# Deeper rings in a linear-attention and gated-convolution kernel: four output buffers, four gates, three x chunks

## The chip, the cores and the metric

The kernel runs on one NeuronCore of a Trainium2 chip. The metric is the time of one execution on the device in microseconds; the median of several runs is compared.

## The reference

All arrays are float32 (the weights of the second block arrive as float64). The first block is a linear attention without softmax, normalised per head; the second one multiplies a value projection by a gate that is the sigmoid of a causal depthwise convolution over time, and projects the product once more.

```python
# q, k, v: (8 batches, 8 heads, 576 tokens, 64)
kv = einsum('bhsd,bhse->bhde', k, v)
o = einsum('bhsd,bhde->bhse', q, kv)
o = o / sqrt(mean(o*o, axis=-1) + 1e-6) * g_norm
x = o.transpose(0, 2, 1, 3).reshape(8, 576, 512)
xp = concatenate([zeros((8, 4, 512)), x], axis=1)
gate = sigmoid(sum(conv_w[t] * xp[:, t:t+576] for t in range(5)))
out = (gate * (x @ w_val)) @ w_out
```

## The kernel before

**Order.** The whole order is written out by hand in the string `PLAN`: some 1,240 steps such as `normalise 3 1`, each a small function of a batch `b` (0 to 7) and a piece of it. The program records the steps in that order, so each engine and each DMA queue runs its own instructions in that order; a tile framework adds the semaphore waits. Nothing is reordered at run time. Batches overlap: while one is projected, the next is in its gate and the one after is loaded.

**One batch.** `load_half` and `load_q` bring k, v and q on SyncE's queue (SP). `kv_product` makes the 64x64 products of k and v, `kv_copy` takes them out of PSUM. `raw_pair` and `raw_tail` multiply the turned q with them; five chunks `c` of tokens result (four of 128 and a tail). `square` (ScalarE), `sums` (VectorE, DVE) and `powers` (GpSimd) make the norm, and `normalise` writes the chunk into a tile `x`: 8 (for the tail 4) ScalarE instructions at L592, for batch 0 one of DVE. The chunk then goes into the transposed array `xT`: for batches 0, 1 and for the tail by PE (`turn_x`) and ScalarE (`keep_x`), otherwise by DVE's 32x32 transposes (`turn_blocks`, L617) and DMAs (`move_blocks`, L625, four a step, half on SP's queue and half on GpSimd's). A buffer of `x` is free again after `turn_x` or `turn_blocks`. `halo` (GpSimd, L632) copies the causal margin inside `xT`.

**Gate.** For each of four blocks `jt` of 128 channels, `gate_start` (ScalarE, L636) writes a new tile `gate`, four `gate_tap` (DVE, L642) add the taps of the convolution, `gate_end` (ScalarE, L649) applies the sigmoid, and `gated` (DVE, L667) multiplies it into the value projection that lies in `gv`. After `gated` the buffer is free.

**Projections.** `val_fast` and `val_keep` make the value projection, by a scheme of seven half-size products in place of eight; the sums that it needs are made by `x_sums` (DVE, L688). The output projection is made by the same scheme: `token_sums` (DVE, L773), `fast_product` (PE, L795) and `fast_keep`, which takes the products out of PSUM into a tile `ot`: ScalarE copies first (L807, L809, L811, L818), and DVE adds the rest (L805). The last 64 tokens of two batches go by `out_product` (PE, L741) and `keep_out` (ScalarE, L749). `store` (L827) sends each `ot` tile out in four DMAs of 64 KB on SP's queue; the buffer is free when they have landed.

**Weights.** They arrive as float64 and are narrowed in the first 70 us by `narrow_weight`; its parts 5 and 6 (DVE, L382 and L387) use buffers of the same ring `ot` as scratch, and part 7 (DVE, L391) is the last reader.

**Rings.** A tile is taken with `work.tile(..., tag=..., bufs=n)`: tiles of one tag share `n` buffers. When a tile is taken, it gets the buffer that has been free for longest in the order of the steps, and its first writer waits for the last user of the tile that held that buffer. So the depth of a ring changes no order, only which earlier instruction the first writer must wait for.

Of the kernel before, what the change touches and what calls it, by code (L numbers as in the profile page):

```python
# [9 lines left out]
FP32 = mybir.dt.float32  # L10
U32 = mybir.dt.uint32
# [4 lines left out]
P = 128  # L16
# [193 lines left out]
def kernel(  # L210
# [13 lines left out]
    C = H * D  # L224
# [17 lines left out]
    FAST_VAL = 2  # L242
    FAST_OUT = 0
    ROOTS = {(0, 2): H + H // 2, (0, 1): 2 * H}
    GATES = 3
    GVS = 3
    assert NJ == 4 and NB == 18
    assert 2 * T == P and NB * TB == S and SV <= 512 and C <= 512 and D == 2 * TB
# [3 lines left out]
    work = ctx.enter_context(tc.tile_pool(name="work", bufs=2))  # L252
# [45 lines left out]
    st = {}  # L298
# [51 lines left out]
    def narrow(key, dst, n):  # L350


        w = staged[key]
        rows, size = w.shape[0], w.shape[1]
        split = lambda a: a if len(dst.shape) == 2 else a.rearrange(
            "p (m c) -> p m c", m=dst.shape[1])
        lo, hi = w[:, :, 0], w[:, :, 1]
        if n in (0, 5, 6):
            tag, kind, bufs = {0: ("wexp", U32, 2), 5: ("ot", U32, 3), 6: ("ot", FP32, 3)}[n]
            staged[key, n] = work.tile(  # L360
                [P, C], kind, tag=tag, bufs=bufs, name=f"{tag}{n}_{key[0]}{key[1]}")[0:rows, 0:size]
        e, m, mf = (staged.get((key, part)) for part in (0, 5, 6))

        if n == 0:
            nc.vector.tensor_scalar(
                out=e, in0=hi, scalar1=20, scalar2=0x7FF,
                op0=ALU.logical_shift_right, op1=ALU.bitwise_and,
            )
        elif n == 1:
            nc.scalar.activation(out=e, in_=e, func=AF.Relu, bias=biases[0:rows, 0:1])  # L370
        elif n == 2:
            nc.scalar.activation(out=e, in_=e, func=AF.Relu, bias=biases[0:rows, 1:2], scale=-1.0)
        elif n == 3:
            nc.scalar.activation(
                out=e, in_=e, func=AF.Identity, bias=biases[0:rows, 2:3], scale=-float(1 << 23))
        elif n == 4:
            nc.vector.scalar_tensor_tensor(
                out=e, in0=hi, scalar=0x80000000, in1=e, op0=ALU.bitwise_and, op1=ALU.bitwise_or,
            )
        elif n == 5:  # L380

            nc.vector.tensor_scalar(  # L382
                out=m, in0=hi, scalar1=0xFFFFF, scalar2=1 << 20,
                op0=ALU.bitwise_and, op1=ALU.bitwise_or,
            )
        elif n == 6:
            nc.vector.scalar_tensor_tensor(  # L387
                out=mf, in0=lo, scalar=2.0 ** -32, in1=m, op0=ALU.mult, op1=ALU.add,
            )
        else:  # L390
            nc.vector.scalar_tensor_tensor(  # L391
                out=dst, in0=split(mf), scalar=gcol[:] if key[0] == "wval" else 2.0 ** -20,
                in1=split(e.bitcast(FP32)),
                op0=ALU.mult, op1=ALU.mult,
            )
# [15 lines left out]
    def narrow_weight(*key):  # L411
        narrow(key[0:2], weights[key[0:2]][3], key[2])
# [130 lines left out]
    def heads(c):  # L543
        return H if c < NJ else H // 2
# [30 lines left out]

    def normalise(b, c):
        n = heads(c)
        x = work.tile([P, C], FP32, tag="x", bufs=2, name=f"x{b}_{c}")
        st["x", b, c] = x
        root = st["rt", b][:, FIRST[c]:FIRST[c] + n]  # L580
        if b in WHOLE:
            nc.vector.tensor_tensor(
                out=x[:, 0:n * D].rearrange("p (r h e) -> p r h e", r=2, e=D),
                in0=st["raw", b, c][:].rearrange("p (h r e) -> p r h e", r=2, e=D),
                in1=root.rearrange("p (h r) -> p r h", r=2).unsqueeze(3).broadcast_to((P, 2, n // 2, D)),
                op=ALU.mult)
            return
        for r, raw in enumerate(st["raw", b, c]):
            if b in ACT_NORM:
                for h in range(n // 2):  # L590
                    to = r * n // 2 + h
                    nc.scalar.activation(  # L592
                        out=x[:, to * D:(to + 1) * D], in_=raw[:, h * D:(h + 1) * D], func=AF.Copy,
                        scale=root[:, to:to + 1])
                continue
            nc.vector.tensor_tensor(
                out=x[:, r * n // 2 * D:(r + 1) * n // 2 * D].rearrange("p (h e) -> p h e", e=D),
                in0=raw.rearrange("p (h e) -> p h e", e=D),
                in1=root[:, r * n // 2:(r + 1) * n // 2].unsqueeze(2).broadcast_to((P, n // 2, D)), op=ALU.mult)
# [34 lines left out]
    def gate_start(b, jt):  # L634
        gate = work.tile([P, S], FP32, tag="gate", bufs=GATES, name=f"gate{b}_{jt}")
        nc.scalar.activation(  # L636
            out=gate[:], in_=xTs[b % 2][:, jt, HALO:SX], func=AF.Copy, scale=cwT[:, K - 1, jt:jt + 1])
        st["gate", b, jt] = gate
# [106 lines left out]
        st["po", i, c] = po  # L745

    def keep_out(i, c):
        ot = work.tile([P, C], FP32, tag="ot", bufs=3, name=f"ot{i}_{c}")
        nc.scalar.copy(out=ot[:], in_=st["po", i, c][:])  # L749
        st["ot", i, c] = ot  # L750

# [47 lines left out]
    def fast_keep(i, p, n):  # L799
        a, b, c = (st.get((bank, i, p)) for bank in "abc")  # L800
        row = int(n in (1, 4, 6))
        if ("ot", i, 2 * p + row) not in st:
            st["ot", i, 2 * p + row] = work.tile([P, C], FP32, tag="ot", bufs=3, name=f"ot{i}_{2 * p + row}")
        first, second = (st.get(("ot", i, 2 * p + r)) for r in range(2))
        add = lambda out, one: nc.vector.tensor_tensor(out=out, in0=one, in1=out, op=ALU.add)  # L805
        if n == 0:
            nc.scalar.copy(out=first[:, LOW], in_=a)  # L807
        elif n == 1:
            nc.scalar.copy(out=second[:, HIGH], in_=c)  # L809
        elif n == 2:  # L810
            nc.scalar.copy(out=first[:, HIGH], in_=a)  # L811
        elif n == 4:
            add(second[:, HIGH], a)
        elif n == 5:
            add(first[:], st["bc", i, p][:].rearrange("p r c -> p (r c)"))
        else:
            last = (i, p) == (B // 2 - 1, 2 * NV - 1)
            (nc.vector.tensor_copy if last else nc.scalar.copy)(out=second[:, LOW], in_=a)  # L818
# [4 lines left out]
    def store(i, c, queue=nc.sync, blocks=range(HB)):  # L823
# [5 lines left out]
    steps = {f.__name__: f for f in (  # L829
        load_half, load_q, load_q_rows, stage_weight, narrow_weight, turn_cw, keep_cw, start_warm, warm_up,  # L830
        kv_product, kv_half, kv_copy, turn_q, turn_q_rows, sort_q, raw_half, raw_pair, raw_tail, square, sums, powers, normalise,
        turn_x, keep_x, turn_blocks, move_blocks, halo, gate_start, gate_tap, gate_end, val_product, keep_val, gated,
        val_sums, x_sums, val_fast, val_keep, out_product, keep_out, weight_sums, token_sums, fast_product, fast_keep,
        store, store_last)}
    with tc.manual_schedule():
# [34 lines left out]
```

## Time and profile before

| | |
|---|---|
| runs shown, median (lowest to highest) | 305.32 us (304.0 to 305.74) |
| the profiled execution, time | 305.54 us |
| its span (first to last instruction) | 303.8 us |
| TensorE: matmuls (PE), weight loads (PEld) | 293.9 us, 226.6 us busy |
| VectorE (DVE) | 273.0 us busy |
| ScalarE (ACT) | 194.4 us busy |
| GpSimd (POOL) | 114.5 us busy |
| DMA | 55.51 MB, mean 183 GB/s |

The profile is of one execution. Its own time is 1.74 us longer than its span. Busy times of engines overlap, so they don't add up to the span. A wait is written with the instruction that waits, an arrow, and the last instruction that it waited for; three numbers behind it are the microseconds in total, how often, and the longest. `SPq` and `PEq` are an engine's queue rather than its arithmetic; "issue" is time in which an engine waited for nothing that the profile shows.

### The profile page before, as it was taken

What the parts mean: (1) busy time and instruction counts of PE and PEld (TensorE: products, weight loads), DVE (VectorE), ACT (ScalarE), POOL (GpSimd) and SP (SyncE); (2) the same over time, 40 slices, a digit from 0 to 9 for tenths busy, and PEclk for the clock granted to TensorE, in tenths of its full rate; (3) what the DMA queues carried; (4) which work ended last, traced back from release to release, by engine and by line L of the source; (5) the groups of instructions that cost most, each with busy time, mean ns of one, the idle gap of its engine ahead of it and who ended that gap; (6) DMA issues with size and microseconds to landing.
All of it is one profiled execution on the core that took longest, in us unless ns stands there. A gap on an engine that the chain in (4) does not pass through costs nothing.

```text
span 303.8 us, 8778 instructions
## 1 busy us (share of the span) xinstructions
PE 293.9 (97%) x3333; PEld 226.6 (75%) x3333; DVE 273.0 (90%) x482; ACT 194.4 (64%) x606; POOL 114.5 (38%) x127
## 2 busy tenths in 40 slices
PE   7998999999999999999999999999999999999993
PEld 4787777777887885777778757787877578888582
DVE  1699999999999999999999999999999999999612
ACT  2799989989568654983586537682888354534220
POOL 3047074326549036265328452245535613000000
PEclk9999999999999999999999999999999999999997
DMA  7999995277559776988589477937411621112423
GB/s 269 397 398 340 271 296 144 58 242 223 165 134 332 212 187 147 286 233 247 153 249 299 125 175 214 311 101 222 108 38 37 175 68 36 35 46 61 104 69 104
DMA packets 32073, 55.51 MB, mean 183 GB/s; under 512 B 6166, under 2 KB 14358, under 8 KB 32032
## 3 DMA queue, kind: packets, MB, share of 16 engines
q1 hardware_dynamic: 29520, 49.76, 56.6%
q0 software_dynamic: 1632, 3.17, 4.0%
q10 hardware_dynamic: 880, 2.03, 1.8%
q8 instruction: 26, 0.43, 0.6%
q14 instruction: 15, 0.12, 0.1%
HBM read 39.21 MB, written 9.44 MB: 160 GB/s over the span
## 4 chain that ended last, share of the span: by engine, by line
PE 76%; DMA 8%; SPq 5%; ACT 4%; DVE 3%; issue 2%; DVEq 0%
PE a L795 15%; PE va L703 13%; PE cb L795 12%; PE val L654 11%; PE vc L703 6%; PE kvps L445 4%; PE raw L521 4%; DMA out_dram<-ot 4%; PE out L741 4%; PE vb L703 3%; DMA qs<-in_q_dram 3%; SPq L625 2%; PE xTps L604 2%; DMA v<-in_v_dram 2%; SPq L322 1%
## 5 line engine op out<-in xcount | busy, mean ns | idle before, releaser
L573 POOL TENSOR_TENSOR rt<-ss,mhalf 128x8 f32<-128x8 f32 (+3 forms) x38 | 68.5, 1810 | 101.0 <-DVE ss L565 100.8
L642 DVE SCALAR_TENSOR_TENSOR gate<-xT,cwT,gate 128x576 f32<-128x576 f32 x128 | 101.8, 809 | 1.0
L592 ACT ACTIVATE x<-raw,rt 128x64 f32<-128x64 f32 x252 | 55.9, 353 | 6.9 <-POOL rt L573 4.1
L625 POOL DMA_DIRECT2D xT<-y x48 | 26.4, 557 | 25.9 <-DVE ot L805 14.4
L654 PE MATMUL val<-xT,wval 128*128 128x288 f32 x128 | 33.4, 412 | 0.0
L795 PE MATMUL a<-wsum,sums 128*128 128x256 f32 x128 | 32.5, 383 | 0.0
L649 ACT ACTIVATE gate<-gate 128x576 f32<-128x576 f32 x32 | 22.0, 692 | 12.1 <-DVE gate L642 11.9
L654 PEld LDWEIGHTS val<-xT,wval 128*128 128x128 f32 x128 | 23.5, 190 | 6.9 <-DVE wval L391 0.5
L795 PEld LDWEIGHTS a<-wsum,sums 128*128 128x128 f32 x128 | 23.9, 190 | 4.4 <-issue 0.6
L556 ACT ACTIVATE sq<-raw 128x256 f32<-128x256 f32 (+1 forms) x70 | 22.1, 402 | 7.8 <-PE raw L521 7.5
L703 PE MATMUL va<-xs,vsum 128*128 128x288 f32 x96 | 26.6, 409 | 0.0
L636 ACT ACTIVATE gate<-xT,cwT 128x576 f32<-128x576 f32 x32 | 25.2, 810 | 1.4 <-DVE gv L667 1.3
L565 DVE TENSOR_REDUCE ss<-sq 128x8 f32<-128x520 f32 (+1 forms) x40 | 24.7, 627 | 0.8 <-ACT sq L556 0.7
L667 DVE TENSOR_TENSOR gv<-gv,gate 128x576 f32<-128x576 f32 x32 | 23.6, 750 | 0.9 <-ACT gate L649 0.8
L703 PEld LDWEIGHTS va<-xs,vsum 128*128 128x128 f32 x96 | 18.0, 190 | 5.2 <-ACT x L592 0.4
L632 POOL COPY xT<-xT 128x124 f32<-128x124 f32 x32 | 17.5, 585 | 10.9 <-ACT xT L611 10.9
L521 PEld LDWEIGHTS raw<-kv,qT 64*64 64x64 f32 x1008 | 16.7, 134 | 6.4 <-issue 3.5
L521 PE MATMUL raw<-kv,qT 64*64 64x64 f32 x1008 | 19.0, 221 | 0.9 <-DVE gv L710 0.6
L445 PEld LDWEIGHTS kvps<-v,k 64*64 64x64 f32 x1008 | 15.8, 135 | 4.1 <-issue 2.9
L445 PE MATMUL kvps<-v,k 64*64 64x64 f32 x1008 | 17.4, 220 | 0.0
L470 DVE STREAM_TRANSPOSE qT<-qs 128x512 f32<-128x512 f32 x24 | 16.6, 693 | 0.5 <-DMA qs<-in_q_dram 0.5
L805 DVE TENSOR_TENSOR ot<-cb,ot 128x512 f32<-128x512 f32 x16 | 10.9, 681 | 6.8 <-DMA out_dram<-ot 4.1
(114 smaller groups left out, 545.5 us busy)
## 6 DMA issues: line engine op xcount, KB each, us to landing
qs<-in_q_dram SPq DMA_DIRECT2D x96, 140.0 KB, 4.6
out_dram<-ot SPq DMA_DIRECT2D x140, 64.0 KB, 1.7
k<-in_k_dram SPq DMA_DIRECT2D x14, 576.0 KB, 6.7
v<-in_v_dram SPq DMA_DIRECT2D x12, 576.0 KB, 7.0
xT<-y SPq DMA_DIRECT2D x48, 64.0 KB, 2.7
xT<-y POOLq DMA_DIRECT2D x48, 64.0 KB, 3.1
y<-in_moe_w_val_dram SPq DMA_DIRECT2D x4, 512.0 KB, 11.4
w_wout<-in_moe_w_out_dram SPq DMA_DIRECT2D x4, 512.0 KB, 7.1
```

What stands on the lines that cost most here:

```text
L445: nc.tensor.matmul(st["kvps", b][s][r * D:(r + 1) * D, i], st["k", b, i][rows, r, cols], st["v", b, i][rows, r, cols], start=(j == 0), sto ...
L521: nc.tensor.matmul(st["raw", b, c][r][cols, to * D:(to + 1) * D], st["qT", b][rows, hp, first:first + D], kvs[b % 2][rows, hp, :], start=T ...
L565: nc.vector.reduce_sum(out=st["ss", b][:, FIRST[c]:FIRST[c] + n], in_=st["sq", b, c][:, 0:n], axis=AX.X)
L573: nc.gpsimd.tensor_tensor(out=st["rt", b][:, which], in0=st["ss", b][:, which], in1=mhalf[:, which], op=ALU.pow)
L592: nc.scalar.activation(out=x[:, to * D:(to + 1) * D], in_=raw[:, h * D:(h + 1) * D], func=AF.Copy, scale=root[:, to:to + 1])
L625: (nc.sync if i % 2 else nc.gpsimd).dma_start(out=xTs[b % 2][i * TB:(i + 1) * TB, :, first:first + P], in_=y[a * TB:(a + 1) * TB, i])
L636: nc.scalar.activation(out=gate[:], in_=xTs[b % 2][:, jt, HALO:SX], func=AF.Copy, scale=cwT[:, K - 1, jt:jt + 1])
L642: nc.vector.scalar_tensor_tensor(out=gate[:], in0=xTs[b % 2][:, jt, tap * TB:tap * TB + S], scalar=cwT[:, tap, jt:jt + 1], in1=gate[:], op ...
L654: nc.tensor.matmul(val[:], wval[:, kc, jt * P:(jt + 1) * P], xTs[b % 2][:, kc, HALO + n * SV:HALO + (n + 1) * SV], start=(kc == 0), stop=( ...
L667: nc.vector.tensor_tensor(out=both, in0=both, in1=st["gate", b, jt][:], op=ALU.mult)
L703: nc.tensor.matmul(st[bank, "val", b, mj][:], weights_[:, k], tokens()[:, k], start=(n in (0, 1, 3) and k == 0), stop=(k == NK // 2 - 1), ...
L795: nc.tensor.matmul(st[bank, i, p], tokens()[:, k], weights_[:, k], start=(n < 2 and k == 0), stop=(k == NK // 2 - 1), skip_group_check=True)
```

## The change

Three rings get one buffer more each: `gate` has four in place of three, `x` three in place of two, `ot` four in place of three (in all four places where a tile of that tag is taken). No step is moved, and every engine keeps its instructions and their order. The buffers take 6,400 more bytes of each SBUF partition; the tiles that lie behind them in the same pool move up by so much.

```diff
-    GATES = 3
+    GATES = 4
...
-            tag, kind, bufs = {0: ("wexp", U32, 2), 5: ("ot", U32, 3), 6: ("ot", FP32, 3)}[n]
+            tag, kind, bufs = {0: ("wexp", U32, 2), 5: ("ot", U32, 4), 6: ("ot", FP32, 4)}[n]
...
-        x = work.tile([P, C], FP32, tag="x", bufs=2, name=f"x{b}_{c}")
+        x = work.tile([P, C], FP32, tag="x", bufs=3, name=f"x{b}_{c}")
...
-        ot = work.tile([P, C], FP32, tag="ot", bufs=3, name=f"ot{i}_{c}")
+        ot = work.tile([P, C], FP32, tag="ot", bufs=4, name=f"ot{i}_{c}")
...
-            st["ot", i, 2 * p + row] = work.tile([P, C], FP32, tag="ot", bufs=3, name=f"ot{i}_{2 * p + row}")
+            st["ot", i, 2 * p + row] = work.tile([P, C], FP32, tag="ot", bufs=4, name=f"ot{i}_{2 * p + row}")
```

## The prediction

> **What bounds the kernel now.** I read the page first, part 1 and the chain in part 4, then the windows, then the list of waits engine by engine, and last the timeline around each wait that a ring can have caused.
>
> ```profile
> PE 293.9 (97%) x3333; PEld 226.6 (75%) x3333; DVE 273.0 (90%) x482; ACT 194.4 (64%) x606; POOL 114.5 (38%) x127
> ...
> PE 76%; DMA 8%; SPq 5%; ACT 4%; DVE 3%; issue 2%; DVEq 0%
> ```
>
> TensorE fills 97% of the span and carries 76% of the chain that ended last. ScalarE, which makes the first write of nearly every tile whose ring grows, is busy for 64% and has 4% of the chain. The windows show whether that average hides a stage with another limit (columns: stretch, its length, then busy time of PE, PEld, DVE, ACT, POOL):
>
> ```profile
> 30.00:60.00 30.00, 29.99 (x464) 23.02 (x463) 29.82 (x51) 28.22 (x84) 11.05 (x9) 1.00 0.71 191
> ...
> 240.00:270.00 30.00, 30.00 (x133) 23.54 (x130) 28.98 (x45) 13.31 (x32) 5.80 (x8) 1.00 0.25 67
> ...
> sum 268.00, PE 266.44 PEld 206.31 DVE 252.47 ACT 173.33 POOL 102.78; mean PE 29.60 PEld 22.92 DVE 28.05 ACT 19.26 POOL 11.42
> ```
>
> From 30 to 298 us PE is busy for 266.44 of 268.00 us, so only 1.56 us are open there. DVE is nearly as full: 29.82 of 30 us in the first stretch, 28.98 in the last one shown. Both run their instructions in a fixed order, so neither can use time that is freed on ScalarE unless it was itself waiting for that.
>
> **Part by part: which waits the rings make.** Nothing is added or removed. The built program has the same instructions in the same order on all five engines; a new tile only waits for the last user of an older tile than before. I looked for these waits by their form: a first writer of the tile (ScalarE at L592 for `x`, L636 for `gate`, L807, L809 and L749 for `ot`; DVE at L382 and L387 for the weights' scratch) that waits for the last user (DVE's turn_blocks or gated; a store's landing). The timeline of ScalarE has these; the bracket is the idle time before and what ended it:
>
> ```profile
> 100.07 1.74 ACT L592 ACTIVATE x<-raw,rt 128x64 f32<-128x64 f32 x8 [1.39 <-DVE y L617]
> 104.72 1.74 ACT L592 ACTIVATE x<-raw,rt 128x64 f32<-128x64 f32 x8 [0.33 <-DVE y L617]
> ...
> 151.55 0.78 ACT L636 ACTIVATE gate<-xT,cwT 128x576 f32<-128x576 f32 x1 [0.36 <-DVE gv L667]
> ...
> 203.76 1.75 ACT L592 ACTIVATE x<-raw,rt 128x64 f32<-128x64 f32 x8 [1.09 <-DVE ot L805]
> ...
> 245.01 0.77 ACT L636 ACTIVATE gate<-xT,cwT 128x576 f32<-128x576 f32 x1 [0.93 <-DVE gv L667]
> 249.29 0.37 ACT L807 COPY ot<-a 128x256 f32<-128x256 f32 x1 [0.99 <-DMA out_dram<-ot]
> 270.21 0.37 ACT L809 COPY ot<-cb 128x256 f32<-128x256 f32 x1 [0.84 <-DMA out_dram<-ot]
> 276.59 0.37 ACT L807 COPY ot<-a 128x256 f32<-128x256 f32 x1 [1.99 <-DMA out_dram<-ot]
> 287.34 0.58 ACT L749 COPY ot<-out 128x512 f32<-128x512 f32 x1 [4.16 <-DMA out_dram<-ot]
> ```
>
> - `x`, two chunks to three: 1.39 + 0.33 + 1.09 = 2.81 us. (At 203.76 the name is another DVE line; DVE's transpose of the chunk that held the buffer had run just before it, from 202.75.)
> - `gate`, three to four: 0.36 + 0.93 = 1.29 us.
> - `ot`, three to four: 0.99 + 0.84 + 1.99 = 3.82 us. The 4.16 us at 287.34 is left out: the matrix product that this copy reads (out_product 3 8) runs on PE from 283.64 for 3.58 us, to 287.22, so it ends the wait whatever the store does.
> - Weights' scratch in the `ot` ring: first writer and last user are both DVE, which runs in order, so a ring there never makes it wait. Zero.
>
> Together 2.81 + 1.29 + 3.82 = 7.92 us, all of it on ScalarE, which has 303.8 - 194.4 = 109.4 us without work. They cost the span only if something full waits for what ScalarE does next. Two examples. After 276.59 ScalarE's next copy, L724 at 276.85, fills a piece of `gv`; DVE, which takes it up in gated, works through its taps without a pause from 275.76 and reaches that step at 278.92, 1.7 us after the copy, and PE runs on. After 100.07 the chunk feeds DVE's transpose; in the 30 us around it DVE is busy for 29.27. If this cover were gone, the bill would be the whole 7.92 us.
>
> The other side is the waits of the engines that are full. For PE's weight loads, 27 to 298 us:
>
> ```profile
> PEld raw L521 <- DVE gv L710: 1.0, 1, 1.0
> ...
> PEld a L795 <- ACT ot L807: 0.4, 1, 0.4
> ...
> PEld raw L521 <- ACT gate L636: 0.4, 1, 0.4
> ...
> PEld va L703 <- ACT x L592: 0.4, 1, 0.4
> ```
>
> Waits that name a line with a grown ring are these three, and three smaller ones (L636 0.3, L592 0.2, L811 0.2): 0.4 + 0.4 + 0.4 + 0.3 + 0.2 + 0.2 = 1.9 us. A weight load runs beside the matmul before it, so most of this lies under a busy PE; of the multiplications themselves hardly any wait is left (the 1.56 us above). The gain therefore lies between 0 and 1.56 us on PE. I take 0.3 us: all load waits that name another engine or a DMA sum to 10.2 us in this list, these six are 1.9 of them, and that share of the idle time is 1.9 / 10.2 x 1.56 = 0.29. DVE's few waits from 60 us to 285 name PE, a load of q, and ScalarE's squares, sigmoids and copies into `gv`, none of them a first write into a grown ring; its 4.1 us for a store at 290.97 stand in the drained end, where PE's product ended only at 290.88.
>
> What is late next: the same PE and DVE as before. The stores do not move up the SP queue's order. An earlier copy into `ot` lets a store go earlier only where DVE's add at L805 follows it at once, and DVE is full.
>
> Sum: the profiled execution is 305.54 us, a span of 303.8 and 1.74 around it. 303.8 - 0.3 = 303.5, and 305.24 in all. It lies 0.22 above the median of the runs (305.32, from 304.0 to 305.74), so for the median I say 305.0 us.
>
> One thing could cost instead: if ScalarE runs ahead, GpSimd's halo copies (L632, 32 of them, 0.585 us each) come earlier and meet other DVE instructions. The rows of DVE's lines (duration min/median/max in ns):
>
> ```profile
> L642 DVE SCALAR_TENSOR_TENSOR gate<-xT,cwT,gate x128: 770/810/837, 30.9 to 280.4; 128x576 f32<-128x576 f32 x128
> ...
> L667 DVE TENSOR_TENSOR gv<-gv,gate x32: 707/749/835, 44.7 to 282.2; 128x576 f32<-128x576 f32 x32
> ...
> L688 DVE TENSOR_TENSOR xs<-xT x12: 739/750/862, 90.7 to 261.2; 128x576 f32<-128x576 f32 x12
> ```
>
> The worst stretch of a two-input instruction is 862 - 750 = 112 ns; of the 128 taps it is 27 ns. Even 32 new meetings at 112 ns would make 3.6 us, and meetings that exist now would go as others come, so I carry zero in the sum, with 3.6 us as its far end. [...]
>
> **The rivals.**
> 1. The PE waits open up: the earlier work on ScalarE also frees PSUM banks sooner, and PE loses all of its 1.56 us and part of the slower joins in its chain. Four matmuls into a or cb take 0.86 us in the chain at best and 1.06 at some 9 places, so up to 2 us more. All of the idle time and a quarter of those: 2.1 us, 302.9 by the span's sum, 303.2 for the median. For it: 7.92 us do go. Against: PE's longest wait, 1.0 us in the raw product, names DVE, not a ring.
> 2. Slower: a load overtakes. q, k and v go on SP's queue, half of the moves xT<-y on GpSimd's. If SP's queue runs ahead because a store was freed, a 576 KB load (7.0 us to land) starts before GpSimd's moves instead of after. In the chain one store already took 8.28 us at 93.50, against a median of 1.7, so such a meeting costs up to 6.6 us; PE's product with the moved xT has next to no slack (a weight load already waits 0.3 us for a move), and the point from which it decides is a move that lands more than some 1.5 us later. At half the price, 3.3 us: 308.6. For it: that stage stands in the chain with DMA and SP. Against: the three `ot` waits over 0.5 us come at 249 us and later, when the last loads are long done; only the 1.39 us of `x` lie near that stage.
> 3. Slower: halo copies on DVE's instructions, at half of the far end, 1.8 us: 307.1. Against: the taps' 27 ns.
> 4. The rings do nothing, since no full engine ever waited for them: 305.3.
>
> **How the numbers follow.** About 0.5% (1.5 us) is what a measurement of this kernel can tell from no change. Forecast, gain of 0 to 1 us: 0.66. Rival 4: 0.10. Both count as the same: 0.76. Rival 1: 0.12, faster. Rival 2: 0.08 and rival 3: 0.04, slower: 0.12. The range has to leave out no more than 0.2: it takes in the forecast, rival 4 and rival 1 (303.2) and goes up to 306.6, for the runs' own spread (305.74 is 0.42 above the median) and the small half of rival 3; rival 2 stays outside. 303.2 to 306.6.
>
> **What would show it.** Right: the eight brackets named above are gone from ScalarE's timeline, its waits for PE and for DVE's taps grow by nearly as much, and PE's busy time from 30 to 298 us stays within 1.5 us of 266.4. Rival 1: PE's gaps shrink and the chain has fewer 1.06 us rows. Rival 2: a PE wait of over 1 us that names xT<-y. Rival 3: medians at L667 and L688 above 780 ns. The forecast is wrong if the span leaves 302.3 to 305.3.

## The result: 0.8 us faster, all of it from the fourth output buffer

Over 15 runs each the changed kernel takes 303.46 us (303.14 to 304.04) and the kernel before 304.25 us (303.67 to 305.74): ratio 0.9973, 95% interval 0.9961 to 0.9984. That is 0.27%, inside the 0.5% that the prediction called the same. The profiled execution has a span of 301.6 us and a time of 303.35 us.

First the page of the changed kernel, engines and chain.

```profile
PE 292.9 (97%) x3333; PEld 226.3 (75%) x3333; DVE 272.7 (90%) x482; ACT 193.8 (64%) x606; POOL 114.1 (38%) x127
...
PE 84%; DVE 6%; ACT 4%; DMA 2%; issue 1%; DVEq 0%; SPq 0%
```

The shares of the engines have not moved. In the chain DMA went from 8% to 2% and SP's queue from 5% to 0%; PE (76% to 84%) and DVE (3% to 6%) took their place. The windows of the changed kernel (stretch, length, then busy time of PE, PEld, DVE, ACT, POOL):

```profile
30.00:60.00 30.00, 29.99 (x464) 23.06 (x463) 29.82 (x53) 28.20 (x85) 11.05 (x9) 1.00 0.74 197
...
240.00:270.00 30.00, 30.00 (x135) 24.55 (x132) 29.17 (x48) 13.36 (x33) 4.20 (x5) 1.00 0.21 56
270.00:298.00 28.00, 26.93 (x121) 20.38 (x119) 16.98 (x27) 8.29 (x20) 0.00 (x0) 1.00 0.31 78
sum 268.00, PE 266.14 PEld 206.32 DVE 252.84 ACT 172.51 POOL 102.44; mean PE 29.57 PEld 22.92 DVE 28.09 ACT 19.17 POOL 11.38
```

The sum misleads: its last stretch ends at 298 us, and the shorter execution is already draining there. The last stretch of the kernel before:

```profile
270.00:298.00 28.00, 27.96 (x126) 21.47 (x125) 17.72 (x31) 8.71 (x21) 0.00 (x0) 1.00 0.28 71
```

Without it, from 30 to 270 us, PE of the changed kernel is busy for 266.14 - 26.93 = 239.21 of 240 us, so 0.79 us are open. The kernel before has 266.44 - 27.96 = 238.48, so 1.52 us are open. PE lost half of its gaps, 0.73 us. That is close to the gain of 0.79 us in the medians, but it isn't the same thing: the two profiled executions differ by 2.2 us in span, and 0.5 us of that lies behind PE's last product, as the section "Where the 0.8 us lie" shows.

ScalarE's timeline of the changed kernel, at the places where the brackets of before stood:

```profile
102.23 0.68 ACT L649 ACTIVATE gate<-gate 128x576 f32<-128x576 f32 x1 [2.80 <-DVE gate L642]
...
202.35 1.74 ACT L592 ACTIVATE x<-raw,rt 128x64 f32<-128x64 f32 x8 [1.08 <-POOL rt L573]
...
249.22 0.37 ACT L811 COPY ot<-a 128x256 f32<-128x256 f32 x1 [1.79 <-PE a L795]
...
270.15 0.37 ACT L818 COPY ot<-a 128x256 f32<-128x256 f32 x1 [2.19 <-PE a L795]
...
277.27 0.37 ACT L811 COPY ot<-a 128x256 f32<-128x256 f32 x1 [2.19 <-PE a L795]
...
285.62 0.58 ACT L749 COPY ot<-out 128x512 f32<-128x512 f32 x1 [4.11 <-PE out L741]
```

No bracket names a ring any more. For seven of the eight the wait itself is gone: ScalarE goes on sooner and stops at its next input instead, PE's product or DVE's taps. The eighth, 1.09 us for the third x chunk, is still there with 1.08 us and now names GpSimd's `powers`. In the kernel before, `powers` ended at 203.72 us and ScalarE started at 203.76, so GpSimd alone would have held it as long. The 4.16 us that named a store near the end are now 4.11 us that name PE, as the prediction said when it left them out.

### The profile page after: what moved, and what is told of

Same layout as the page of the kernel before. It is cut to its first block, busy times and chain, and to the rows that moved or that the text cites. A ratio compares the mean times of both kernels' runs of the same rounds, so it can differ in the third digit from the quotient of the medians.

```text
span 301.6 us, 8766 instructions
## 1 busy us (share of the span) xinstructions
PE 292.9 (97%) x3333; PEld 226.3 (75%) x3333; DVE 272.7 (90%) x482; ACT 193.8 (64%) x606; POOL 114.1 (38%) x127
## 3 DMA queue, kind: packets, MB, share of 16 engines
q10 hardware_dynamic: 880, 2.03, 1.8%
## 4 chain that ended last, share of the span: by engine, by line
PE 84%; DVE 6%; ACT 4%; DMA 2%; issue 1%; DVEq 0%; SPq 0%
PE a L795 18%; PE cb L795 14%; PE va L703 13%; PE val L654 11%; PE vc L703 6%; PE raw L521 5%; PE kvps L445 5%; PE out L741 5%; PE vb L703 4%; PE xTps L604 2%; DMA qs<-in_q_dram 2%; DVE gate L642 2%; DVE xs L688 1%; ACT sq L552 1%; PE qTps L485 1%
## 5 line engine op out<-in xcount | busy, mean ns | idle before, releaser
L642 DVE SCALAR_TENSOR_TENSOR gate<-xT,cwT,gate 128x576 f32<-128x576 f32 x128 | 101.9, 810 | 1.0
L649 ACT ACTIVATE gate<-gate 128x576 f32<-128x576 f32 x32 | 22.0, 692 | 13.4 <-DVE gate L642 13.1
L667 DVE TENSOR_TENSOR gv<-gv,gate 128x576 f32<-128x576 f32 x32 | 23.6, 751 | 0.9 <-ACT gate L649 0.8
L632 POOL COPY xT<-xT 128x124 f32<-128x124 f32 x32 | 17.1, 574 | 9.8 <-ACT xT L611 9.8
L795 PE MATMUL cb<-wsum,sums 128*128 128x256 f32 x64 | 16.8, 386 | 0.0
L795 PE MATMUL cb<-wout,gv 128*128 128x256 f32 x64 | 16.8, 385 | 0.0
```

The costliest lines, as they stand in the source:

```text
L642: nc.vector.scalar_tensor_tensor(out=gate[:], in0=xTs[b % 2][:, jt, tap * TB:tap * TB + S], scalar=cwT[:, tap, jt:jt + 1], in1=gate[:], op ...
L667: nc.vector.tensor_tensor(out=both, in0=both, in1=st["gate", b, jt][:], op=ALU.mult)
L795: nc.tensor.matmul(st[bank, i, p], tokens()[:, k], weights_[:, k], start=(n < 2 and k == 0), stop=(k == NK // 2 - 1), skip_group_check=True)
```

## The experiments

Every kernel was timed in five rounds beside the kernel before, whose median in the three groups was 304.18, 304.26 and 304.31 us.

**Which ring?** First the kernel before against itself, to see what a comparison can tell.

> The kernel before once more, as a null. Theory R (the rings: each microsecond saved is a wait of ScalarE that a ring ended): ratio 1.000 within 0.1%, and its profile shows the same two stalls as the first one, the q load at about 115 us that DVE waits for (0.5 us) and the raw product at 122 us (0.6 to 0.7 us on PE). Theory C (accidents: the profiled stalls at 64, 115 and 122 us are drawn anew in each execution): ratio 1.000 too, but at least one of the three stalls is missing or moved. In both the PE gap of 0.37 us at 64 us, which names no releaser, may come or go: no ring has its wait there.

Measured: 304.44 us, ratio 1.0003 (0.9991 to 1.0016). So 0.15% can be told from nothing. Its profile has the gap of PE at 64 us (0.60 us), but neither DVE's wait for q at 115 us nor PE's wait at 122 us, as Theory C said: such stalls come and go between executions of one kernel.

The third x chunk alone:

```diff
-        x = work.tile([P, C], FP32, tag="x", bufs=2, name=f"x{b}_{c}")
+        x = work.tile([P, C], FP32, tag="x", bufs=3, name=f"x{b}_{c}")
```

> Only the third x chunk. Theory R by place: the saving of the full change lies in steps, about 0.5 us between 112 and 122 us (behind the x waits at 100 and 105 us) and 0.24 us at 245 to 249 us (behind a gate wait and a store). So x alone gives about 0.5 us: ratio 0.998, and the DVE wait for q at 115 us is gone. By shares of the removed waits (2.81 of 7.92 us) it would be 0.3 us, 0.999. Theory L (layout: the tiles behind the rings moved): some part of 0.8 us by chance of address, no relation to the x waits, which vanish all the same.

Measured: 304.51 us, 1.0014 (1.0001 to 1.0026), so neither the 0.5 nor the 0.3 us came. The fourth gate alone:

```diff
-    GATES = 3
+    GATES = 4
```

> Only the fourth gate. Theory R by place: about 0.24 us or nothing (the step at 245 us), ratio 0.999 to 1.000; ScalarE's wait of 0.93 us at 245 us is gone, those for x and for stores stay. By shares (1.29 of 7.92 us): 0.13 us. Theory L: as for x.

Measured: 304.53 us, 1.0009 (0.9998 to 1.0020). The fourth output buffer alone (the same edit at L748 and L803):

```diff
-            tag, kind, bufs = {0: ("wexp", U32, 2), 5: ("ot", U32, 3), 6: ("ot", FP32, 3)}[n]
+            tag, kind, bufs = {0: ("wexp", U32, 2), 5: ("ot", U32, 4), 6: ("ot", FP32, 4)}[n]
```

> Only the fourth output buffer. Theory R by place: 0 to 0.24 us, ratio 0.999 to 1.000; ScalarE's waits for stores at 249, 270 and 277 us are gone, the x waits stay. By shares (3.82 of 7.92 us): 0.4 us, the largest of the three. Theory L: as for x.

Measured: 303.45 us (303.19 to 303.94), 0.9978 (0.9970 to 0.9987). This one edit has the whole gain, more than the 0.24 us by place and the 0.4 us by shares. It was confirmed from the other side by the full change without it, the x and gate edits together:

> The full change without the fourth output buffer. Theory R: no gain, 0.999 to 1.001, since the third x chunk and the fourth gate gave none alone; the x and gate waits are gone from ScalarE all the same. Sum of the two alone (0.14% and 0.09% slower): 1.002. Theory F: 1.000 if the instruction block before the stall at 64 us comes after 61 us, 0.998 if it comes before.

Measured: 304.46 us, 1.0004 (0.9986 to 1.0023). Three us of waits on ScalarE (1.39 + 0.33 for x, 0.36 + 0.93 for the gate) vanish for nothing.

**Is it where the tiles lie?** The rings stay as before, but an unused tile of a buffer's size stands beside each ring, so that the tiles behind move as in the change (`pad` takes one such tile, once; `pad_x` and `pad_gate` stand behind the other two rings):

```diff
-    staged = {}
+    staged = {}; pad = lambda tag, n: st.setdefault(tag, None) or st.update({tag: work.tile([P, n], FP32, tag=tag, bufs=1, name=tag)})
...
+        tag == "ot" and pad("pad_ot", C)
...
+        pad("pad_x", C)
...
+        pad("pad_gate", S)
```

> The rings of before, with three unused tiles beside them, so that every tile behind the rings lies where the full change puts it; instructions, order and waits are those of before. Theory R (the output ring's waits): 1.000, and the stall of PE at 64 us (0.6 to 0.9 us in both profiles of before) stays. Theory L (layout of the data): up to the whole gain, 0.997 to 0.998, and the stall at 64 us is gone. Theory F (PE's own instruction blocks of 16 KB come too late at 64 us, at 61.4 to 61.7 us instead of 57): 1.000 if the addresses of data don't matter to it.

Measured: 304.21 us, 1.0000 (0.9982 to 1.0018). The place of the tiles does nothing that could be told.

**Is it the fetching of PE's instructions?** Four profiles with three output buffers (before, before again, x alone, pad) have a gap in the raw product at 64 us that names no releaser; gate alone, x and gate, and the changed kernel and output alone don't. The page of the profile has a DMA queue of instructions (`q8 instruction: 26, 0.43`, 26 transfers and 0.43 MB), about one block per 256 multiplications and weight loads (6,666 / 26), so I take it for PE's program. The last block before 64 us was fetched at 61.1 to 61.7 us where the gap is, at 57 us in the two with four buffers and in x and gate, and at 60.3 in gate alone. So two kernels with 40 tiny multiplications more at the start, to move the block borders: the kernel before, and the one with four output buffers.

```diff
-start_warm 5 256;
+start_warm 5 256; start_warm 40 32;
```

> The rings of before, with 40 tiny extra multiplications on PE between 3 and 6 us, where it waits for the first load: they move the borders of PE's instruction blocks by 80 instructions, towards earlier steps. Theory F: the block that came at 61.6 us, in the middle of a raw product, is asked for near 57 us; the stall at 64 us goes, 0.998 (another block may fall badly and give some back). Theory R: 1.000, the stall at 64 us stays or goes without effect on the time.

> The fourth output buffer alone, with the same 40 tiny multiplications. Theory F: the same time as before with the shift, within 0.1%, since neither has the stall at 64 us. Theory R: 0.22% faster than before with the shift, as without it (0.9978 against 1.000).

Measured: 306.54 us, 1.0074 (1.0046 to 1.0102), and 305.49 us, 1.0034 (1.0018 to 1.0049). The pages now have 27 transfers on that queue. The 64-us gap is gone in both profiles, and the fourth buffer is still worth 306.54 - 305.49 = 1.05 us. So the gain doesn't rest on that gap. Both theories missed what the shift itself costs, 306.54 - 304.26 = 2.3 us; why it does is not shown.

**Is it the landing of old stores?** Four more kernels. Five output buffers (5 for 4 in the edit above):

> Five output buffers, gates and x as before. Theory R (the gain is that ScalarE's copies into the output tiles no longer wait for the landing of an old store): with four buffers no such wait was left, so the fifth has nothing to take away: 303.3 to 303.7 us, ratio 0.9975 to 0.999 to the kernel before, the same as four. Theory D (the depth of the ring acts in another way, such as where tiles lie or how the weights' scratch rotates): another value than with four, by 0.3 us or more.

Measured: 303.52 us, 0.9980 (0.9962 to 0.9998): the same as four. The weights' scratch in a ring of its own, output tiles with three:

```diff
-            tag, kind, bufs = {0: ("wexp", U32, 2), 5: ("ot", U32, 3), 6: ("ot", FP32, 3)}[n]
+            tag, kind, bufs = {0: ("wexp", U32, 2), 5: ("ots", U32, 3), 6: ("ots", FP32, 3)}[n]
```

> The weights' scratch (parts 5 and 6 of the narrowing) gets a ring of three of its own; the output tiles keep three buffers. Theory R: the scratch is done by 70 us and the first output tile comes later, so the waits for store landings after 200 us are all there: 304.0 to 304.6 us, ratio 0.999 to 1.001. Theory S (the fourth buffer helped the scratch in the first 70 us): 303.3 to 303.8 us, ratio about 0.998.

Measured: 304.19 us, 0.9999 (0.9988 to 1.0011). It isn't the scratch. Then stores that land later, with three and with four buffers:

```diff
-            queue.dma_start(out=rows_out[2 * i + bb, n], in_=ot[j * TB:(j + 1) * TB, :])
+            for r in ((0, TB // 2), (TB // 2, TB)) if i in (1, 2) else ((0, TB),): queue.dma_start(out=rows_out[2 * i + bb, n, r[0]:r[1]], in_=ot[j * TB + r[0]:j * TB + r[1], :])
```

> Three output buffers, and the stores of the second and third pair of batches go out as eight DMAs of 32 KB in place of four of 64 KB. At 0.42 us an issue on SP's queue a store's last landing comes some 1.7 us later. Theory R: each of ScalarE's 4 to 6 waits for a landing from 211 to 250 us grows by up to 1.7 us, and those that had 0.3 to 0.4 us on PE now have 1 to 2: 306 to 310 us. Theory A (the landings never mattered; the 0.8 us come from elsewhere): within 0.5 us of the kernel before.

> The same eight DMAs of 32 KB, with four output buffers. Theory R: the copy now waits for a store that is one tile older, which has several microseconds more, so the later landing is hidden: 303.3 to 304.2 us, no wait of ScalarE for out_dram<-ot between 200 and 280 us, and 2 us or more below the same stores with three buffers. Theory A, or a cost of the extra issues on SP's queue: as slow as the same stores with three buffers.

Measured: three buffers 327.05 us, 1.0767 (1.0728 to 1.0806); four buffers 314.73 us, 1.0330 (1.0299 to 1.0361). The direction is that of Theory R: with later landings the fourth buffer is worth some 12 us (327.05 - 314.73) instead of 0.8. Both sizes were missed: I expected 306 to 310 and 303.3 to 304.2. Three readings say why. ScalarE's and PE's timelines with three buffers and split stores:

```profile
215.53 0.37 ACT L807 COPY ot<-a 128x256 f32<-128x256 f32 x1 [4.06 <-DMA out_dram<-ot]
222.06 0.37 ACT L809 COPY ot<-cb 128x256 f32<-128x256 f32 x1 [4.53 <-DMA out_dram<-ot]
```

```profile
222.49 2.08 PE L795 MATMUL cb<-wout,gv 128*128 128x256 f32 x4 [3.18 <-ACT ot L809]
224.35 3.83 PE L795 MATMUL a<-wsum,sums 128*128 128x256 f32 x8
```

The copy at 222.06 waited 4.53 us for a store, and PE's next product into that PSUM bank waited 3.18 us for the copy and started 0.06 us after it ended. That is the path on which a ring on ScalarE reaches PE: landing, copy out of PSUM, next product in the same bank. The first three of ScalarE's waits for a store grew from 2.91 (at 208.64 us) to 4.06 and 4.53 us; that late copies make late adds and late stores in turn would explain it, but is not shown. Second, PE did not come back at full speed: eight multiplications took 3.83 us behind the gap; the same eight with four buffers and whole stores:

```profile
215.76 1.89 PE L795 MATMUL a<-wsum,sums 128*128 128x256 f32 x8
```

The windows of the kernel with three buffers and split stores show that PE was busy for only 62.18 of 75 us, and from 220 to 230 us the clock (the granted clock is the third number from the end):

```profile
195.00:270.00 75.00, 62.18 (x525) 46.66 (x524) 55.88 (x92) 36.72 (x121) 27.99 (x32) 0.91 0.41 108
220.00:230.00 10.00, 7.51 (x21) 5.79 (x22) 4.32 (x7) 5.27 (x19) 3.68 (x2) 0.66 0.29 73
```

The two times differ by a factor of 3.83 / 1.89 = 2.03. The granted clock was 0.97 from 220 to 222 us, 0.50 from 222 to 228 and 0.82 from 228 to 230; by the clock's own record it was 0.50 for 6.83 us, from 221.89. In the split kernel with four buffers it was 0.50 for 3.41 us, from 217.10. Not every gap had it: behind the one of 1.76 us at 215.95 us, with three buffers and split stores, the clock was 1.00 (216 to 220 us). What sets it off and what ends it is not shown.

Third, the issues themselves. The split kernel with four buffers, DVE's and ScalarE's timelines and SP's queue:

```profile
213.81 0.71 DVE L470 STREAM_TRANSPOSE qT<-qs 128x512 f32<-128x512 f32 x1 [5.35 <-DMA qs<-in_q_dram]
```

```profile
211.96 0.37 ACT L807 COPY ot<-a 128x256 f32<-128x256 f32 x1 [2.73 <-DMA qs<-in_q_dram]
216.09 0.37 ACT L809 COPY ot<-cb 128x256 f32<-128x256 f32 x1 [2.11 <-DMA out_dram<-ot]
222.58 0.37 ACT L807 COPY ot<-a 128x256 f32<-128x256 f32 x1 [3.93 <-DMA out_dram<-ot]
```

```profile
207.94 2.78 SPq L322 DMA_DIRECT2D qs<-in_q_dram  x4
210.82 3.92 SPq L827 DMA_DIRECT2D out_dram<-ot  x8
```

With whole stores and four buffers the same load of q goes out earlier, and in less time:

```profile
203.17 1.78 SPq L322 DMA_DIRECT2D qs<-in_q_dram  x4
```

With split stores the load stands behind six stores, issued from 204.78 to 207.84 us; with whole stores it stands behind four, from 201.35 to 203.08. DVE stood 5.35 us for it. So the split costs 314.73 - 303.45 = 11.3 us even with the deeper ring; these rows are the part of it that I can name, and my expectation "no wait for a landing" failed too. The pair shows that landings reach PE through the ring, and how steep that is once they do; it doesn't give the 0.8 us.

## Where the 0.8 us lie

PE's open time (length less busy time) from the same two windows in every profile with whole stores, and the time from the end of PE's last product to the end of the span:

| kernel | output buffers | 30 to 195 us | 195 to 270 us | behind the last product | median of runs |
|---|---|---|---|---|---|
| before | 3 | 1.28 | 0.24 | 5.11 | 304.25 |
| before again | 3 | 1.08 | 0.45 | 5.11 | 304.44 |
| x alone | 3 | 1.15 | 0.21 | 5.07 | 304.51 |
| gate alone | 3 | 1.37 | 0.25 | 5.10 | 304.53 |
| pad | 3 | 0.92 | 0.80 | 5.10 | 304.21 |
| x and gate | 3 | 0.98 | 0.25 | 5.13 | 304.46 |
| scratch apart | 3 | 1.79 | 0.24 | 5.05 | 304.19 |
| before, shifted | 3 | 1.04 | 0.24 | 5.07 | 306.54 |
| changed kernel | 4 | 0.57 | 0.21 | 4.60 | 303.46 |
| output alone | 4 | 0.57 | 0.21 | 4.59 | 303.45 |
| five buffers | 5 | 0.53 | 0.21 | 4.59 | 303.52 |
| output alone, shifted | 4 | 0.74 | 0.24 | 4.56 | 305.49 |

Leave the shifted pair aside first. With three buffers PE has 1.57 us open on the mean of the seven, with four or five 0.77: 0.80 us less. That this equals the difference of the medians is chance, for the spans of these profiled executions differ by 1.61 us on the mean (303.07 against 301.46): 1.11 us up to the end of the last product, of which the 0.80 are a part, and 0.51 us behind it. The profiled executions with three buffers are up to 1.3 us slower than the medians of their runs, those with four or five 0.1 to 0.3 us faster, so the parts of the profiles can't be put on the medians one by one.

**Behind the last product: 0.5 us in every profile.** This part doesn't change from execution to execution: 5.05 to 5.13 us in all eight profiles with three buffers, 4.56 to 4.60 in all four with four or five. In the shifted pair it is nearly the whole difference of the two spans, 0.51 of 0.55 us. The last two output tiles go out there, half on SP's queue and half on ScalarE's (`store_last` in the plan). In these traces the operands of a store name the semaphore that its landing raises. The issues of two of SP's last four stores, before and then after the change:

```profile
300.45 0.32 SPq L827 DMA_DIRECT2D out_dram<-ot  x1
300.81 0.45 SPq L827 DMA_DIRECT2D out_dram<-ot  x1
```

```profile
297.74 0.38 SPq L827 DMA_DIRECT2D out_dram<-ot  x1
298.75 0.32 SPq L827 DMA_DIRECT2D out_dram<-ot  x1
```

The last product ended at 298.65 and 296.97 us, so these issues come 1.80 and 2.16 us behind it before, 0.77 and 1.79 us after. Before, the first of the two uses the same semaphore as ScalarE's first store, issued at 298.60 us; SP waits for it at 300.40, and that store landed at 300.39. After, only the second one shares a semaphore with ScalarE's first store: issued at 296.92, landed at 298.74, SP goes on at 298.75. The last landing moves from 3.95 to 3.44 us behind the last product.

The number of buffers as such doesn't do it: the split kernel with four buffers has ScalarE's first store and SP's third on one semaphore, as the kernel before has, and needs 5.29 us behind its last product, like the split kernel with three (5.28). In the kernel before and the changed one the first 319 of SP's 325 DMAs have the same semaphores; why the deeper ring changes the last ones is not shown. If the executions without a profile are alike here, 0.5 of the 0.79 us are this, and about 0.3 us are left for PE.

**Behind 195 us the path is visible.** The kernel before, profiled a second time, on ScalarE and on PE:

```profile
211.54 0.37 ACT L807 COPY ot<-a 128x256 f32<-128x256 f32 x1 [1.52 <-DMA out_dram<-ot]
225.25 0.37 ACT L809 COPY ot<-cb 128x256 f32<-128x256 f32 x1 [1.52 <-DMA out_dram<-ot]
248.95 0.37 ACT L807 COPY ot<-a 128x256 f32<-128x256 f32 x1 [1.20 <-DMA out_dram<-ot]
```

```profile
249.38 1.99 PE L795 MATMUL a<-wsum,sums 128*128 128x256 f32 x8 [0.17 <-ACT ot L807]
```

The waits at 211 and 225 us are not in the first profile of the same kernel. A wait at one or more places from 210 to 226 us stands in six of the eight profiles with three buffers and whole stores (the shifted one included), and in none with four or five. Mostly PE is covered; at times it isn't, as in pad:

```profile
217.39 0.37 ACT L807 COPY ot<-a 128x256 f32<-128x256 f32 x1 [1.09 <-DMA out_dram<-ot]
```

```profile
217.82 1.13 PE L795 MATMUL a<-wsum,sums 128*128 128x256 f32 x4 [0.56 <-ACT ot L807]
```

By the open time this part is 0 to 0.6 us an execution, 0.14 on the mean of the unshifted rows (0.35 against 0.21).

**Ahead of 195 us it isn't.** The larger part of the open time, 1.22 against 0.56 us, has other names: the 64-us gap, a wait of the raw product for `gv` at 121 or 122 us, in the scratch kernel a load of k (1.1 us). No profile has a wait of ScalarE for a store there. One thing that the deeper ring changes on a full engine is DVE's waiting instructions at L805, before and after:

```profile
L805 DVEq EVENT_SEMAPHORE  x51: 21/50/4669, 85.4 to 297.2; - x51
```

```profile
L805 DVEq EVENT_SEMAPHORE  x42: 21/50/5017, 84.6 to 295.5; - x42
```

Nine of them at a median of 50 ns are 0.45 us of DVE's queue, of which I can't show that any reached the end. Why each execution with three buffers loses something in these 165 us, at a different place each time, and the unshifted ones with four or five lose the same 0.53 to 0.57, stays open. So does the 64-us gap: no kernel here took it away alone. It follows the fetch rather than the number of buffers: in the profiles without the shift it stands where the last block before 64 us was fetched at 61.1 us or later (five, the split kernel with three buffers among them), 0.07 us are open in the scratch kernel, with the block at 60.8, and nothing where it came at 60.4 or earlier (six, two of them with three buffers).

## Why the prediction was right or wrong

- **The bound: right.** PE is at 97% before and after, and DVE stays as full.
- **The removed waits: right for seven of eight.** The 1.09 us at 203.76 were not the ring's, since GpSimd held ScalarE as long; x has 1.72 us in place of 2.81, and the sum is 6.83 in place of 7.92. From the lists of waits, ScalarE's waits for the taps (L649) and for PE at L811, L818 and L724 grew by 1.2, 1.5, 0.9 and 1.5 us, 5.1 of the 6.83.
- **x, gate and scratch at nothing: right**, shown by x alone, gate alone, both together, and the scratch apart.
- **The output ring at 0.3 us: the mis-sized term.** It was worth 0.8. The end of the kernel stood in the sum with nothing: the prediction looked there at DVE's add, which PE did end, and held that SP's queue keeps its order. It does, but two of the last four issues came 1.0 and 0.4 us sooner behind the last product, and this is 0.5 us in every profile. About 0.3 us are left for PE if the executions without a profile are alike there; that this is the forecast is luck. I took the ring's share of all load waits in one profile (1.9 of 10.2) times PE's 1.56 us; in the two profiles compared, half of those 1.56 us went. The share was counted by the name in a list of one execution; other executions of the same kernel have store waits on ScalarE at 211 and 225 us, where that one has none. "The three `ot` waits over 0.5 us come at 249 us and later" holds for one execution, not for the kernel.
- **"The same instructions": too broad.** The arithmetic and the DMAs are the same, but a wait that needs an instruction of its own is one too: 51 became 42 at L805. And the last stores got other semaphores, so they waited for other landings.
- **The base.** The predicted 305.0 stood on a median of 305.32 from three runs. Over 15 runs it is 304.25. Of the miss of 1.54 us this is 1.07, and the ring's term with the rounding is the rest. The span of 301.6 fell outside 302.3 to 305.3, so by its own last sign the forecast was wrong. The reason is for the most part the same: the profiled execution of before, 305.54 us, was 1.3 us above its median of 15.
- **Rival 1** gave a time close to the measured one, 303.2, from a base 1 us too high. Its gain of 2.1 us didn't come: PE kept 0.8 us of gaps, and in the chain the joins at 1.06 us did not become fewer (8 before, 10 after). Its "302.9 by the span's sum" doesn't follow either: 303.8 - 2.1 + 1.74 is 303.4.
- **Rivals 2 and 3** did not come: no PE wait of 1 us names xT<-y, and DVE's rows stayed (medians before and after: L667 749 and 751 ns, L688 750 and 751, L642 810 and 811). A DVE instruction took longer beside GpSimd's copies at L632 in the trace of before: the four at L688 that ran beside one took 834 to 862 ns, the eleven with no GpSimd instruction beside them 739 to 758. The copies kept their range too, 277 to 907 ns before and 276 to 907 after. But rival 2's mechanism, SP's order, is real: the split stores kept a load of q back, in a kernel that became 11.3 us slower.
- **Rival 4**, the rings do nothing, is right for two of the three.

## What to carry to other kernels

A ring that a DMA must free is judged by several executions: landings vary (ScalarE waited for a store at 211 and 225 us in one profile of the kernel before, 1.52 us each, and not in the other), so its cost comes and goes, and a single profile can miss it. Follow the path from the landing to the copy out of PSUM to the next product in that bank, and test each ring alone: one more output buffer had the whole gain here, a fifth and two other rings nothing. Look at the end of the kernel too: some 0.5 of the 0.8 us lay in the order of waits of the last stores, which no wait of a tile's first writer shows. And compare gaps with spans of the same executions, not with medians of others. Before stores are cut smaller, count the issues on their queue and name the loads behind them.

## What the runs showed of the hardware

- A gap of PE cost more than its length: in the split kernel with three buffers the 3.18 us at 222 us were followed by multiplications at half speed (3.83 us for eight against 1.89), with a granted clock of 0.66 from 220 to 230 us, 0.50 in each window from 222 to 228.
- A store's issue waited for a store on another queue: in the kernel before SP stood until 300.40 us for the landing (300.39) of a store that ScalarE had issued at 298.60, since both used one semaphore.
- What I take for PE's instructions arrived as 26 transfers of 0.43 MB in all (27 with 40 multiplications more), and a gap without a releaser (0.26 to 0.60 us at 64 us) went with a transfer at 61.1 us or later in all five profiles that have it.
- Forty tiny multiplications put into the start cost 306.54 - 304.26 = 2.3 us, though in the kernel before PE has only ten warm-up multiplications there (L433, 1.36 to 5.84 us) and then waits 0.21 us for the first load of q.
